# Quadrant matmuls for the token rows, and score blocks without the masked quarter, in a fused retention, expert and feed-forward kernel

## The chip, the core and the metric

The kernel runs on one core of a Trainium2 chip. The metric is device time in microseconds (us) from start to end of one execution; the median of several is quoted. The engines are named as the profile names them: PE is TensorE (PEld its weight loads), DVE VectorE, ACT ScalarE, POOL GpSimd, SP the engine that issues most DMAs.

## What is computed

Three layers in a row: a retention layer over 8 batches of 576 tokens with 8 heads of 64, a layer of 8 experts that sends each token to one expert, and a feed-forward layer with a cosine gate. The change lies in the first layer and in what leads from it into the second.

```python
scores = scale * np.matmul(q, k.transpose(0, 1, 3, 2))
Dmat = np.where(rel >= 0, gamma[:, None, None] ** rel[None, :, :], 0.0)
attn = np.matmul(scores * Dmat[None], v)                 # [B, H, S, 64]
x = attn.transpose(0, 2, 1, 3).reshape(B * S, H * 64)    # token rows
logits = x @ w_gate                                      # 8 experts
expert_idx = np.argmax(logits, axis=1)
# each token: relu(x @ w1[e]) @ w2[e], times the softmax weight of its expert
# then h = x @ w_in; (h * cos(h)) @ w_out
```

`rel` is the query's position less the key's, so of a block of 128 keys by 128 queries the entries with a key after the query are zero: below the diagonal nothing counts, and the quarter of the last 64 keys by the first 64 queries is zero as a whole.

## The kernel before

A batch of 576 tokens is cut into five chunks, four of 128 tokens and one of 64 (`CH`, `NCH` = 5), so the first layer is 40 steps, i = 0 to 39. A chunk's keys and queries lie turned (head dimension on the partitions), two heads on top of each other: partitions 0 to 63 hold the even head of a pair j, 64 to 127 the odd one. Per step the parts are:

- `load(i)` (L438 for a full chunk, 1 MB in one DMA; L440 and L441 for the half one) fills one of five `ld` buffers. It is issued on SP at the end of step i - 4, behind the store of the token rows, and its buffer comes free when `intra(i - 5)` has read it.
- `decay(i)` (L449): eight ACT multiplications, one a head, of the values v by the powers of gamma, into `vs`.
- `scores(i)` (L462): keys times queries, 16 matmuls of 64 rows by 64 columns and 128 moving columns (8 of 64 for a half chunk), spread over the array's four quadrants; the even heads go into one PSUM bank, the odd ones into another. DVE multiplies both by the mask into `pT` (L466).
- `inter(i)` (L487, not for a batch's first chunk): the state of the chunks before, `sbd`, times the queries. `intra(i)` (L497, L506): `vs` times `pT` into the same bank pair `xp`, DVE's multiplication into `xt` (L500), then the new state `S`, which ACT copies to `sbd` (L509).
- `rows(i)` (L518): 4 full-array matmuls with 136 moving columns, `xt` against `wgi`, which holds an identity and the gate's weights side by side. Out of it come the token rows (ACT copy `xs`, L520, then the store L523 into `xd`) and partial logits (DVE sum `lgt`, L521).
- `route`, `place`, `spread`, `table`: once per batch, the choice of an expert and the places of the tokens, on DVE, POOL and a little PE. The first expert's weights (`wst`, `wunit`) are loaded and split in the same steps 6 to 28.

Nothing reorders instructions: each engine runs them in the order in which the code emits them, and a step emits `scores(i)`, `decay(i + 1)`, `inter(i - 1)`, `intra(i - 1)`, `rows(i - 2)`, the routing, `load(i + 4)`. Scores and rows take turns in four PSUM banks (tag `sc`). Every fp32 matmul stands in the trace as two records, each with a weight load of its own; so 16 matmuls are 32 records.

At the start SP loads the first chunks in pieces, 13 matmuls on a cleared tile (`warm`, L211) run until the first chunk is there, and `wgi` is put together on DVE (L391 to L395).

## Time and profile before

| | us |
|---|---|
| median of 3 runs | 1379.56 (1375.28 to 1381.71) |
| profiled execution | 1377.58 |
| its span, first to last instruction | 1375.3 |
| PE busy | 1354.1 (98%) |
| DVE, ACT, POOL busy | 939.5 (68%), 757.2 (55%), 191.0 (14%) |
| DMA queue of SP | 256 MB, 53.0% of the 16 engines' span |

The span is one execution; the 2.3 us around it are start and end. PE's share is counted from records that overlap, so a busy PE can still be one that has less to do than its share says. The first layer ends at about 174 us, where the first expert's matmuls begin. From there PE is the engine that everything waits for. In the first layer PE, DVE, ACT and the DMA engines are all above three quarters, so there the shares alone don't tell which of them sets the pace.

### The profile page before, as it was taken

What the parts mean: (1) busy time and instruction counts of PE and PEld (TensorE: products, weight loads), DVE (VectorE), ACT (ScalarE), POOL (GpSimd) and SP (SyncE); (2) the same over time, 40 slices, a digit from 0 to 9 for tenths busy, and PEclk for the clock granted to TensorE, in tenths of its full rate; (3) what the DMA queues carried; (4) which work ended last, traced back from release to release, by engine and by line L of the source; (5) the groups of instructions that cost most, each with busy time, mean ns of one, the idle gap of its engine ahead of it and who ended that gap; (6) DMA issues with size and microseconds to landing.
All of it is one profiled execution on the core that took longest, in us unless ns stands there. A gap on an engine that the chain in (4) does not pass through costs nothing.

```text
span 1375.3 us, 28314 instructions
## 1 busy us (share of the span) xinstructions
PE 1354.1 (98%) x11234; PEld 1262.5 (92%) x11234; DVE 939.5 (68%) x1928; ACT 757.2 (55%) x1687; POOL 191.0 (14%) x300
## 2 busy tenths in 40 slices
PE   7999999999999999999999999999999999999998
PEld 6888899999999999998999999999999999999997
DVE  4777865867778687847666676766767676666655
ACT  5788725444544455336556555555555555555544
POOL 4334530121211212100010100101001010010101
PEclk9999999999999999999999999999999999999999
DMA  8899626575876668976564655646455564564551
GB/s 290 320 329 346 213 61 217 180 262 183 285 246 203 211 230 268 331 275 259 176 258 164 220 190 191 220 166 249 183 192 201 194 233 161 209 226 162 196 184 57
DMA packets 72648, 300.58 MB, mean 219 GB/s; under 512 B 7748, under 2 KB 15904, under 8 KB 58560
## 3 DMA queue, kind: packets, MB, share of 16 engines
q1 hardware_dynamic: 60000, 256.18, 53.0%
q0 software_dynamic: 12512, 42.56, 8.3%
q8 instruction: 89, 1.46, 0.4%
q14 instruction: 47, 0.39, 0.1%
HBM read 247.24 MB, written 51.47 MB: 217 GB/s over the span
## 4 chain that ended last, share of the span: by engine, by line
PE 49%; issue 6%; POOL 0%; POOLq 0%; ACT 0%
PE acc L1341 25%; PE hps L1265 24%; POOL out_dram L1323 0%; POOLq L1430 0%; ACT ka L1295 0%; POOL spare L159 0%; PE acc L1352 0%; POOLq L1323 0%; ACT orow L1321 0%
## 5 line engine op out<-in xcount | busy, mean ns | idle before, releaser
L1341 PE MATMUL acc<-wunit,gh 128*128 128x512 f32 x1152 | 358.2, 392 | 0.0
L1265 PEld LDWEIGHTS hps<-far,wquad 128*128 128x128 f32 x2064 | 261.8, 191 | 8.0 <-ACTq L1239 0.7
L1265 PE MATMUL hps<-far,wquad 128*128 128x256 f32 x2064 | 266.7, 283 | 0.5 <-ACTq L1239 0.5
L1341 PEld LDWEIGHTS acc<-wunit,gh 128*128 128x128 f32 x1152 | 207.2, 189 | 36.0
L1341 PE MATMUL acc<-wunit,gl 128*128 128x512 f32 x576 | 224.3, 389 | 0.0
L274 PE MATMUL hps<-xT,wunit 128*128 128x256 f32 (+6 forms) x1536 | 209.4, 297 | 0.5 <-ACT yev L291 0.5
L274 PEld LDWEIGHTS hps<-xT,wunit 128*128 128x128 f32 x1536 | 206.7, 188 | 0.9 <-ACT yev L291 0.7
L289 PE MATMUL hps<-hh,wunit 128*128 128x256 f32 (+6 forms) x960 | 197.9, 301 | 0.0
L289 PEld LDWEIGHTS hps<-hh,wunit 128*128 128x128 f32 x960 | 155.8, 190 | 0.1
L289 PE MATMUL hps<-hl,wunit 128*128 128x256 f32 (+6 forms) x480 | 143.5, 299 | 1.4 <-DVE hl L278 1.4
L1323 POOL DMA_INDIRECT out_dram<-orow,perm x36 | 35.4, 982 | 740.3 <-DVE orow L1319 736.4
L1341 PEld LDWEIGHTS acc<-wunit,gl 128*128 128x128 f32 x576 | 108.2, 188 | 24.5 <-DVE gl L1308 0.8
L1306 ACT CAST gh<-sa 128x512 fp32r<-128x512 f32 x144 | 89.6, 622 | 72.9 <-DVE sa L1302 72.9
L1302 DVE SCALAR_TENSOR_TENSOR sa<-sa,box 128x512 f32<-128x512 f32 x144 | 99.0, 688 | 42.8 <-ACT sa L1300 41.7
L1265 PE MATMUL hps<-near,wquad 128*128 128x256 f32 x960 | 126.6, 283 | 0.0
L1265 PEld LDWEIGHTS hps<-near,wquad 128*128 128x128 f32 x960 | 123.1, 191 | 3.6
L1276 DVE TENSOR_TENSOR box<-hps,box 128x256 f32<-128x256 f32 x72 | 30.6, 424 | 136.7 <-PE hps L1265 136.5
L1308 DVE TENSOR_TENSOR gl<-sa,gh 128x512 fp32r<-128x512 f32 x144 | 98.9, 687 | 18.5 <-ACT gh L1306 12.9
L1297 DVE SCALAR_TENSOR_TENSOR sa<-box,ka 128x512 f32<-128x512 f32 x144 | 98.9, 687 | 12.4 <-ACT ka L1295 12.3
L1275 ACT COPY box<-hps 128x256 f32<-128x256 f32 x72 | 26.8, 372 | 141.3 <-PE hps L1265 132.5
L1021 DVE TENSOR_TENSOR wunit<-wst,wunit 128x512 fp32r<-128x512 f32 x112 | 75.2, 686 | 36.9 <-ACT wunit L1020 36.8
L1299 ACT ACTIVATE sa<-sa 128x512 f32<-128x512 f32 x144 | 91.2, 634 | 8.6 <-DVE sa L1297 8.6
(217 smaller groups left out, 1877.4 us busy)
## 6 DMA issues: line engine op xcount, KB each, us to landing
wquad<-ws SPq DMA_DIRECT2D x72, 1792.0 KB
wst<-in_moe_w_dram SPq DMA_DIRECT2D x64, 512.0 KB
ld<-in_full_dram SPq DMA_DIRECT2D x29, 1024.0 KB
ws<-cvo POOLq DMA_DIRECT2D x28, 512.0 KB, 3.5
xd<-xs SPq DMA_DIRECT2D x32, 256.0 KB
cvw<-in_moe_w_in_dram SPq DMA_DIRECT2D x16, 512.0 KB
cvw<-in_moe_w_out_dram SPq DMA_DIRECT2D x16, 512.0 KB
wd<-cvo POOLq DMA_DIRECT2D x16, 512.0 KB, 5.3
```

Of the source, the lines that this page charges most:

```text
L274: mm(out=ph[:, :n], lhsT=u[:, a, kc, f0:f0 + P], rhs=t[:, bq, kc, :n], start=(idx == 0), stop=(idx == 11))
L289: mm(out=py[:, :n], lhsT=u[:, w], rhs=t[:, :n], start=(fc == 0 and g == 0), stop=(fc == 7 and g == 2))
L1021: nc.vector.tensor_sub(out=u[:, 1, 2 * g + c], in0=s[:, c], in1=u[:, 0, 2 * g + c])
L1265: mm(out=o, lhsT=u[:, s, kc, a], rhs=x[:, bq, kc], start=(s in (0, 1, 2) and idx == 0), stop=(idx == 5), skip_group_check=True)
L1276: nc.vector.tensor_add(out=u2, in0=y[:, :HT], in1=p1)
L1297: nc.vector.scalar_tensor_tensor(out=sa, in0=x, scalar=INV2PI, in1=ka, op0=ALU.mult, op1=ALU.subtract)
L1299: nc.scalar.activation(out=sa, in_=sa, func=AF.Sin, scale=math.pi)
L1302: nc.vector.scalar_tensor_tensor(out=sa, in0=sa, scalar=-1.0, in1=x, op0=ALU.add, op1=ALU.mult)
L1306: nc.scalar.copy(out=gh, in_=sa)
L1308: nc.vector.tensor_sub(out=gl, in0=sa, in1=gh)
L1323: ins = nc.gpsimd.indirect_dma_start(out=out[:, :], out_offset=bass.IndirectOffsetOnAxis(ap=perm[:, k:k + 1], axis=0), in_=o, in_offset=None)
L1341: mm(out=acc2[T][c], lhsT=pair[n][:, fh, c % 2 * P:(c % 2 + 1) * P], rhs=u[:, w, fc % 4], start=(q == 0 and fh == 0 and n == 0 and w == 0) ...
```

## The change

- `scores` of a full chunk leaves out the masked quarter: the last 64 keys are multiplied with the last 64 queries alone, 64 moving columns in place of 128. For every second pair of heads the two halves of the keys (and of the values and decays that belong to them) are swapped, on the host and in the tables, so that in each group of four matmuls all quadrants carry the same number of columns. The mask gets a second, swapped form. What stands in the quarter not written is multiplied by zero; so four named PSUM banks are cleared at the start and handed round (`next_bank`) in place of the pool's buffers.
- `rows` is done by head in the quadrants: 16 matmuls (8 for a half chunk) of 64 rows by 64 columns with 72 moving columns (64 of an identity and 8 of the gate) in place of 4 with 136. Token rows come out in plain head order, and the expert's first weights are laid in that order on the host. `wgi` is built on the host and loaded.
- `rows(i - 2)` is emitted right behind `decay(i + 1)`, ahead of `inter(i - 1)`; `rows(38)` ahead of `inter(39)`.
- `decay` is shared: from step 3 on, ACT does four heads one by one and POOL the other four in one instruction; for the first three chunks DVE does all eight in one, in the step itself.
- At the start the load of chunk 1's keys and queries goes ahead of chunk 0's values, a one-element ACT instruction brings the table load forward, and six more `warm` matmuls follow `scores(0)`.

```diff
...
+        banks = [ps1.tile([P, 4, P], F32, name=f"bank{i}") for i in range(4)]
+        for t in banks:
+            nc.vector.memset(t, 0.0)
+        def next_bank():
+            banks.append(banks.pop(0))
+            return banks[-1]
...
         def decay(i):
-            for h in range(H):
+            h0 = 0 if i < OWN else H // 2
+            for h in range(h0):
                 nc.scalar.mul(vs[:n, h], s["v"][:n, h], cc(C_GK + c * H + h, 1, n))
+            (nc.vector if i < OWN else nc.gpsimd).tensor_tensor(
+                out=vs[:n, h0:], in0=s["v"][:n, h0:],
+                in1=cc(C_GK + c * H + h0, H - h0, n).unsqueeze(2).to_broadcast([n, H - h0, D]), op=ALU.mult)
...
-            scs = [ps1.tile([P, 4, P], F32, tag="sc", name="sc", bufs=4) for g in range(2)]
+            scs = [next_bank() for g in range(2)]
...
+                for j0 in (0, 2):
+                    for late in range(2):
+                        for j in (j0, j0 + 1):
+                            r = D * (j % 2 ^ late)
+                            for g in range(2):
+                                mm(out=scs[g][r:r + D, j, D * late:], lhsT=kT[D * g:D * g + D, j, r:r + D],
+                                   rhs=qT[D * g:D * g + D, j, D * late:], start=(j0 == 0 and not late), stop=True,
+                                   skip_group_check=True)
...
         def rows(i):
+            two = [next_bank().rearrange("p j t -> p (j t)")[
+                :, :4 * RW].rearrange("p (j f) -> p j f", f=RW) for g in range(2)]
+            for j in range(4):
+                for g, r in ((0, 0), (1, D), (0, D), (1, 0)):
+                    if r < n:
+                        mm(out=two[g][r:r + D, j, :], lhsT=xt[D * g:D * g + D, j, r:r + D],
+                           rhs=wgi[D * g:D * g + D, j, :], start=(j == 0), stop=True, skip_group_check=True)
             for g in range(2):
-                two = ps1.tile([P, 4, P], F32, tag="sc", name="rw", bufs=4).rearrange("p (j a) t -> p j (a t)", a=2)
-                for j in range(2):
-                    mm(out=two[:, j, 0:RW], lhsT=xts[i % 3][:, 2 * g + j, :], rhs=wgi[:, 2 * g + j, :], start=(j == 0),
-                       stop=True, skip_group_check=True)
-                for j in range(2):
-                    mm(out=two[:, j, 0:RW], lhsT=xts[i % 3][:, 2 * g + j, :], rhs=wgi[:, 2 * g + j, :], start=(j == 0),
-                       stop=True, skip_group_check=True)
...
             scores(i)
-            if i + 1 < NS:
+            if i < OWN:
+                decay(i)
+            if i == 0:
+                warm(NWARM // 2, blank, idle)
+            if OWN <= i + 1 < NS:
                 decay(i + 1)
-            if i == 1:
-                setup_rows()
+            if i >= 2:
+                rows(i - 2)
...
             if i >= 1:
                 inter(i - 1)
                 intra(i - 1)
...
-            if i >= 2:
-                rows(i - 2)
```

On PE, one full step as it stood before: scores, state, values, new state, and the token rows last.

```order
L462 MATMUL sc<-ld 64x128 x16
L487 MATMUL xps<-ld,sbd_136 64x128 x8
L497 MATMUL xps<-pT,vs 64x128 x8
L506 MATMUL S<-vs,ld 64x64 x8
L518 MATMUL rw<-wgi,xt_130 128x136 x4
L462 MATMUL sc<-ld 64x64 x8
```

On PE now, the piece from the end of a step's rows (L566) to the scores of the next step, a half one (L494).

```order
L566 MATMUL bank_149<-wgi,xt_131 64x72
L566 MATMUL bank_150<-wgi,xt_131 64x72
L532 MATMUL xps<-ld,sbd_136 64x128 x8
L542 MATMUL xps<-pT,vs 64x128 x8
L551 MATMUL S<-vs,ld 64x64 x8
L494 MATMUL bank_147<-ld 64x64
L494 MATMUL bank_148<-ld 64x64
```

The rows now stand between scores and state, so the new state is followed at once by the next scores, and rows of chunk i - 2 wait for DVE's `xt` of the step just before.

On DVE, a step with `spread` before: masks, `xt`, the sums of the logits, then the spread's small instructions.

```order
L466 TENSOR_TENSOR pT<-sc,ca 128x4x128 x2
L500 TENSOR_TENSOR xt_132<-xps,gx 128x512
L521 TENSOR_REDUCE lgt_140<-rw 128x8 x2
L605 TENSOR_REDUCE rm<-dd 128x5
L618 TENSOR_REDUCE gts<-ex 128x5
```

The same step on DVE now.

```order
L511 TENSOR_TENSOR pT<-bank_147,ca 128x4x128
L511 TENSOR_TENSOR pT<-bank_148,ca 128x4x128
L570 TENSOR_REDUCE lgt_139<-bank_149 128x8
L570 TENSOR_REDUCE lgt_139<-bank_150 128x8
L545 TENSOR_TENSOR xt_131<-xps,gx 128x512
L654 TENSOR_REDUCE rm<-dd 128x5
```

The sums of the logits, which wait for ACT's copies, have moved ahead of `xt`.

On POOL, once per batch, the chain of the placing before.

```order
L584 TENSOR_TENSOR dd<-dd,hot 128x200
L608 TENSOR_SCALAR tokc<-ct 128x5
L609 TENSOR_TENSOR rt<-hot,tokc 128x5x40
L612 TENSOR_SCALAR oh<-ca,rm 128x128 x5
L626 TENSOR_TENSOR rt<-hot,gh 128x5x40
L626 TENSOR_TENSOR rt<-hot,gl 128x5x40
L575 TENSOR_TENSOR dd<-dsts,ca 128x200
```

The same place on POOL now.

```order
L633 TENSOR_TENSOR dd<-dd,hot 128x200
L478 TENSOR_TENSOR halfv_142<-ld,ca 64x256
L657 TENSOR_SCALAR tokc<-ct 128x5
L658 TENSOR_TENSOR rt<-hot,tokc 128x5x40
L661 TENSOR_SCALAR oh<-ca,rm 128x128 x5
L675 TENSOR_TENSOR rt<-hot,gh 128x5x40
L675 TENSOR_TENSOR rt<-hot,gl 128x5x40
L478 TENSOR_TENSOR vs<-ld,ca 128x256 x4
```

POOL's halves of `decay` (L478) stand between the pieces of that chain.

## Rows read from the trace of the kernel before

**Rows 1.** Windows of 100 us, 170 to 1370 us, their sum: length, busy time.

```profile
sum 1200.00, PE 1195.48 PEld 1120.88 DVE 820.16 ACT 630.83 POOL 117.44; mean PE 99.62 PEld 93.41 DVE 68.35 ACT 52.57 POOL 9.79
```

**Rows 2.** Windows, one per batch of five steps: length, busy, PEclk, DMA share, GB/s.

```profile
28.97:47.61 18.64, 18.64 (x400) 16.98 (x399) 14.19 (x47) 13.84 (x53) 5.83 (x11) 1.00 0.90 315
47.61:70.20 22.59, 20.38 (x406) 17.98 (x405) 15.82 (x47) 16.86 (x63) 7.85 (x15) 1.00 0.91 324
...
89.99:109.79 19.80, 19.55 (x405) 17.68 (x405) 15.73 (x47) 16.54 (x59) 8.53 (x16) 1.00 0.92 326
109.79:129.48 19.69, 19.69 (x405) 17.75 (x405) 15.72 (x47) 16.30 (x59) 8.34 (x15) 1.00 0.97 351
129.48:148.97 19.50, 19.50 (x406) 17.70 (x406) 15.93 (x51) 16.19 (x59) 8.14 (x15) 1.00 0.88 306
```

**Rows 3.** Timeline of PE, one full step: start, length, line, tiles, shape, records.

```profile
102.04 1.10 PE L462 MATMUL sc<-ld 64*64 64x128 f32 x32
102.96 0.62 PE L487 MATMUL xps<-ld,sbd 64*64 64x128 f32 x16
103.51 1.09 PE L497 MATMUL xps<-pT,vs 128*64 128x128 f32 x16
104.44 0.64 PE L506 MATMUL S<-vs,ld 128*64 128x64 f32 x16
105.00 1.19 PE L518 MATMUL rw<-wgi,xt 128*128 128x136 f32 x8
106.12 0.27 PE L462 MATMUL sc<-ld 64*64 64x64 f32 x2
```

**Rows 4.** Narrow windows, L462 (128 columns), then L487 (64): (x) is records in flight.

```profile
109.98:110.00 0.02, 0.02 (x8) 0.02 (x6) 1.00 0.99 410
110.08:110.10 0.02, 0.02 (x12) 0.02 (x8) 1.00 0.26 102
...
110.73:110.75 0.02, 0.02 (x4) 0.02 (x8) 1.00 0.97 410
110.85:110.87 0.02, 0.02 (x12) 0.02 (x11) 1.00 0.00 0
```

**Rows 5.** Groups of instructions, 109.79 to 129.48: count, busy, mean ns, idle before.

```profile
L466 DVE TENSOR_TENSOR pT<-sc,ca 128x512 f32<-128x512 f32 x8 | 5.1, 678 | 0.0
L521 DVE TENSOR_REDUCE lgt<-rw 128x8 f32<-128x16 f32 (+1 forms) x10 | 1.7, 173 | 3.4 <-ACT xs L520 3.4
L449 ACT ACTIVATE vs<-ld,ca 128x64 f32<-128x64 f32 x32 | 8.1, 338 | 1.5 <-DMA ld<-in_full_dram 1.5
L520 ACT COPY xs<-rw 128x256 f32<-128x256 f32 (+1 forms) x11 | 4.1, 371 | 1.0 <-PE rw L518 0.2
L584 POOL TENSOR_TENSOR dd<-dd,hot 128x200 f32<-128x200 f32 x1 | 0.6, 610 | 0.1
```

**Rows 6.** The window of 4 us with the highest rate.

```profile
84.00:88.00 4.00, 4.00 (x84) 3.63 (x82) 3.53 (x12) 3.29 (x13) 3.58 (x8) 1.00 1.04 408
```

**Rows 7.** Timeline: two loads' issues and the decays that waited for them; waits, 20 to 160 us.

```profile
49.49 1.33 SPq L438 DMA_DIRECT2D ld<-in_full_dram  x1
60.46 0.82 ACT L449 ACTIVATE vs<-ld,ca 128x64 f32<-128x64 f32 x3 [3.57 <-DMA ld<-in_full_dram]
...
110.71 0.38 SPq L438 DMA_DIRECT2D ld<-in_full_dram  x1
118.82 2.02 ACT L449 ACTIVATE vs<-ld,ca 128x64 f32<-128x64 f32 x8 [1.06 <-DMA ld<-in_full_dram]
...
ACT vs L449 <- DMA ld<-in_full_dram: 13.6, 12, 3.6
```

**Rows 8.** Timeline of the start.

```profile
0.87 1.45 POOL L405 MEMSET xt<- 128x512 f32 x3
...
18.98 2.02 ACT L449 ACTIVATE vs<-ld,ca 128x64 f32<-128x64 f32 x8 [1.01 <-DMA ld<-in_full_dram]
...
22.15 0.62 PE L487 MATMUL xps<-ld,sbd 64*64 64x128 f32 x16
```

## The prediction

> **What bounds the kernel now.** I read the windows first, then the timeline of one step, then the waits of the engines next to PE.

> Behind the first layer PE is busy 1195.5 of 1200 us [rows 1], and the change does not touch what it does there. So what the first layer saves or loses goes one to one into the end. The base of the sum is the profiled execution, 1377.58 us; the median of the runs is 1379.56, 0.14% above it. A measurement of this kernel can tell about 0.5% from no change: below 1372.7 is faster, above 1386.5 slower.

> In the first layer the windows of a batch [rows 2] show that PE has no idle time in the fifth and sixth batch (19.69 of 19.69, 19.50 of 19.50), and .25 in the fourth; the granted clock is 1.00, even in the second batch, where PE was idle for 2.2 us. So PE sets the pace. Close behind come ACT (16.3 of 19.7), DVE (15.7) and the DMA engines (.88 to .97, 306 to 351 GB/s). That is the case in which a faster PE soon meets something else. Seven batches start between 28.97 and about 168.5; the third, between the second's end and the fourth's start, took 19.8, and the seventh I take as the sixth. Sum: 18.64 + 22.59 + 19.80 + 19.80 + 19.69 + 19.50 + 19.50 = 139.5 us. The second is 2.8 us longer than its like.

> **PE's part.** A full step takes 4.08 us from scores to scores: scores .92, state .55, values .93, new state .56, rows 1.12 [rows 3].

> Records in the quadrants start four together. With 128 moving columns the next four follow about .10 us later (from 8 to 12 in flight in .10); with 64 columns two fours come in .12, so .06 a four [rows 4]. The new scores of a full chunk are 4 fours with 128 columns and 4 with 64, so 4 x (.11 - .06) = .2 us go, .92 becomes .72. The new rows are 8 fours (16 matmuls, two records each) with 72 columns. By .06 x 72/64 a four costs .064, eight cost .51 instead of 1.12, so .61 go. A half chunk's scores don't change; its rows I count like a full one's, since the old ones were 4 full matmuls too. Per batch 4 x .2 + 5 x .61 = 3.85: PE alone would need 19.69 - 3.85 = 15.84 us. Eight batches give 31 us, the most PE can return.

> Moving `rows` next to `scores` also puts two quadrant shapes side by side. I count nothing for it. There are a quarter more PE instructions in a step (records 176 before, 224 now); no row has a price for fetching them, and I bound it by nothing and the 2.8 us of the second batch.

> [...]

> **DVE.** Its masks, `xt` and sums keep their sizes. A batch has 15.7 us of them, and the 3.4 us that it idles ahead of `lgt` it spends waiting for ACT's `xs` [rows 5]. With small gaps the floor is 16.0 to 16.2 us, just above PE's 15.84. In the new order `lgt` stands ahead of `xt`, and `rows(i - 2)` waits for the `xt` of the step just before. So ACT's `xs`, which stands behind `decay`, which waits for a load, now reaches PE by way of DVE within a step.

> **ACT and POOL.** Half the decays leave ACT: (8.1 for full chunks + 2.0 for the half one)/2 = 5.05 us a batch, leaving 11.3 of 16.3 busy. POOL takes them: a row of 128 x 200 takes .61 [rows 5], so 128 x 256 some .78, and 5 of them 3.9 on 8.3, far from full. Only the chain of the placing gets longer: `rm` on DVE waits for POOL's `dd`, which now may stand behind one decay. Bound: nothing, or one POOL decay (.78) a batch, 5 us in all, if DVE has no slack; I take nothing, as DVE waits for ACT anyway, and keep the 5 for the range.

> **The loads.** The highest rate of the trace is 408 GB/s in 4 us at a share of 1.04 [rows 6]. A batch that also carries two loads of `wst` moves 19.69 x 351 = 6.91 MB (the first, third and fifth of the seven), one with a single `wst` load 6.45 (second, fourth), one without 5.97 (sixth, seventh). At 408 the heavy one takes 16.9 us; at the 351 that it reached, 19.7. So the bytes alone leave room for 2.8 us or for none.

> What decides is latency. `load(i + 4)` can go only when the new state of chunk i - 1 has read its buffer, at the end of step i. The timeline has a load whose issue took from 110.71 to 111.09, and whose decay started at 118.82, having waited for it 1.06 us: L = 7.7 us behind the issue. ACT waited 12 times for such loads, 13.6 us together [rows 7]; before, this was off the path. Behind the landing now come, in step i + 3 and ahead of `rows(i + 2)` in step i + 4: half a decay, about 1.0 (2.02 for eight), two `xs` copies .75 (371 ns), two sums .35 (173 ns), `xt` .68 (like `pT`) [rows 5, 7], 2.8 in all; with the issue (.38) 3.2, with hand-offs 3.3. The scores of that step (.72) lie in between in the change's favour; I leave them as reserve. Three steps must hold it: 3T = L + 3.3. With L = 7.7 T is 3.67 and a heavy batch 18.3 us. I scale L with a batch's bytes: 7.2 and 17.5 for a medium batch, 6.65 and 16.6 for a light one. The heavy one then moves 378 GB/s, inside what [rows 6] shows.

> **The start.** Four cleared banks stand ahead of the tile that `warm` reads. Clearing 128 x 512 three times took 1.45 us on POOL. But the first steps wait for loads: the decay of chunk 3 starts at 18.98, when its load is there, and the third step's state matmuls start at 22.15 [rows 8]. The new order of the first loads helps chunk 0, not chunk 3. I take a gain of .6 (one step's rows), with -1.0 and +2.9 as bounds: the loss if chunk 3's load lands later by as much as ACT waits for it there (1.01), the gain if the clearing now beside it (twice 1.45) came free.

> **The sum.** 3 x 18.3 + 2 x 17.5 + 2 x 16.6 = 123.1 against 139.5, a gain of 16.4. The second batch keeps its stall, so 2.8 come back. Start .6, and the last two rows 2 x .61 = 1.2. 1377.6 - 16.4 + 2.8 - .6 - 1.2 = **1362.2 us**. L half a us shorter or longer moves T by .17, thus 35 steps by 6 us: 1356 to 1368.

> **Rivals.** *A, the forecast*: loads set the pace through ACT and DVE. For it: the twelve waits. Chance .50.

> *B, loads keep up and DVE sets the pace*: 7 x 16.2 = 113.4, a gain of 26.1 and 1.8 for start and end, 1350. For it: 408 GB/s in [rows 6], and a load issued sooner may land sooner. Against it: the heavy batches would have to hold 426 GB/s for 16.2 us. PE alone would end at about 1346. Chance .23.

> *C, loads don't come faster at all*: heavy batches stay at 19.7, medium at 19.8, light ones fall to 17.0 (5.97 MB at 351). Gain 5.0 + 1.8: 1371. For it: shares of .97 and above, where the queue is full. Against: [rows 6]. Chance .15.

> *D, the change doesn't shorten the records*: their starts have a least distance, and fewer columns don't bring them closer. The scores' 32 records in .92 are 29 ns each. If that were such a floor, scores would save nothing, rows 1.12 - .92 = .20, PE's batch be 18.7, and eight batches with the start give 1369. Against it: 15 ns in [rows 4]. Chance .06. [...]

> *E, slower*: PE used to pass over a late load, since rows stood a whole step behind `xt`; now `lgt` ahead of `xt` and the closer `rows` carry it to PE. This decides where L exceeds 3 x 4.08 - 3.3 = 8.9. One load was issued by 50.82 and its decay ran at 60.46, L = 9.6, ACT having idled 3.57 [rows 7]; if L stayed there, T would be 4.3, 35 steps would lose .2 each, and the end be 1385; with L = 10, 1390. Against it: that was a single load in the batch with the stall; 7.7 is more like the others. Chance .06.

> **How the numbers follow.** A has the largest chance: 1362. The range takes in B's nearer edge and C: 1348 to 1371; outside are D's and E's slow ends and the half of B in which PE's pace is met. Faster by the bound: nearly all of A, B and D, and two thirds of C, .87; the same: the rest of C, an E with L near 9, .08; slower: E, .05.

> **What would show it.** [...] Batches of 16.6 to 18.3 us, heavy ones longer than light ones, PE idle 1 to 2.5 us in them, DVE's idle still ahead of `lgt`, ACT waiting for `ld` (A). All batches at 16.2 with DVE busy throughout (B). Heavy batches unchanged at 350 GB/s with a share of 1 (C). PE idle, steps above 4.08 (E). Wrong would be the forecast above all if L is not fixed but shrinks with less queueing, or if POOL's halves hold up `vs` or `rm`: then waits on POOL would head DVE's or PE's list.

## The result, and the profile after

The changed kernel takes **1398.51 us** (median of 4 runs, 1396.05 to 1401.81) beside 1378.40 of the kernel before on the same chip: ratio 1.0132, interval 1.0111 to 1.0154. It is 20 us slower; the forecast was 1362, the range 1348 to 1371. The profiled execution has a span of 1400.0 us against 1375.3, so 24.7 us stand to be explained in it.

Where they lie shows in the start of each batch's first new state (first record of `S`, L506 before and L551 now; the last state is taken at the last record of `S`):

| | before | after | more |
|---|---|---|---|
| from the start to the second batch's `S` | 33.94 | 38.05 | 4.1 |
| six batches, second to eighth | 121.0 (20.2 each) | 135.8 (22.6 each) | 14.8 |
| from there to the last state | 13.4 | 16.1 | 2.7 |
| from the last state to the end | 1207.0 | 1210.1 | 3.1 |

The first view is the windows of four batches in a row, as in [rows 2]: length, busy time of PE, PEld, DVE, ACT and POOL with counts, PEclk, DMA share, GB/s.

```profile
63.70:87.20 23.50, 19.29 (x514) 17.61 (x512) 16.53 (x47) 11.14 (x38) 11.15 (x19) 0.85 0.83 293
87.20:109.70 22.50, 18.78 (x514) 17.13 (x510) 16.20 (x47) 11.13 (x38) 11.26 (x19) 0.87 0.77 283
109.70:131.80 22.10, 18.04 (x510) 16.49 (x508) 16.66 (x47) 11.13 (x38) 11.21 (x19) 0.90 0.85 295
131.80:154.90 23.10, 19.15 (x512) 17.55 (x510) 16.26 (x47) 11.14 (x38) 11.17 (x19) 0.86 0.81 291
```

No engine is full any more, the DMA engines move less per second than before, and the granted clock, 1.00 in every batch of [rows 2], is .85 to .90: part of each batch ran at half of it. In the windows of 81 to 86, 105 to 110, 128 to 131 and 149 to 154 us it is .50. What PE waits for is in the list of its waits, 20 to 180 us (total, times, longest):

```profile
PE bank L566 <- issue: 14.8, 6, 3.2
PE bank L494 <- issue: 10.2, 7, 2.2
PE S L551 <- issue: 1.6, 1, 1.6
PE bank L566 <- DVE xt L545: 1.6, 1, 1.6
```

"issue" is time in which PE waits for nothing that the profile shows: 26.6 us in 14 gaps. Only one gap is a wait for `xt`. The timeline of PE shows such a gap and what follows (start, length, line, tiles, shape, records, idle before):

```profile
99.51 0.41 PE L566 MATMUL bank<-wgi,xt 64*64 64x72 f32 x10
102.62 0.54 PE L566 MATMUL bank<-wgi,xt 64*64 64x72 f32 x20 [2.70 <-issue]
...
104.05 1.51 PE L686 MATMUL lg<-rt,oh 128*128 128x120 f32 x5
105.48 1.56 PE L505 MATMUL bank<-ld 64*64 64x128 f32 x32
106.81 1.17 PE L566 MATMUL bank<-wgi,xt 64*64 64x72 f32 x16
107.92 1.97 PE L542 MATMUL xps<-pT,vs 128*64 128x128 f32 x16
```

PE stops in the middle of a line, after 10 of 32 records whose operands are all there, for 2.7 us; then the same lines take nearly twice as long as at a granted clock of 1.00, the values 1.97 us where they take 1.10 below. The gap is one cost, the half clock that follows a second. A step without a gap is as the forecast had it:

```profile
114.19 0.90 PE L505 MATMUL bank<-ld 64*64 64x128 f32 x32
114.91 0.68 PE L566 MATMUL bank<-wgi,xt 64*64 64x72 f32 x32
115.42 0.62 PE L532 MATMUL xps<-ld,sbd 64*64 64x128 f32 x16
115.96 1.10 PE L542 MATMUL xps<-pT,vs 128*64 128x128 f32 x16
116.89 0.64 PE L551 MATMUL S<-vs,ld 128*64 128x64 f32 x16
117.45 0.33 PE L494 MATMUL bank<-ld 64*64 64x64 f32 x4
```

Scores .72, rows .51, the whole step 3.26 us against 4.08 [rows 3]. PE's arithmetic did become faster by what was claimed. (One slip ahead of the prediction: token rows don't come out in plain head order but in the array's, with the heads of pairs 1 and 3 swapped; the first weights are laid to match.)

### The profile page after: what moved, and what is told of

It is laid out like the page before. It is cut to its first block, busy times and chain, and to the rows that moved or that the text cites. A ratio compares the mean times of both kernels' runs of the same rounds, so it can differ in the third digit from the quotient of the medians.

```text
span 1400.0 us, 29955 instructions
## 1 busy us (share of the span) xinstructions
PE 1345.9 (96%) x12072; PEld 1255.3 (90%) x12072; DVE 946.9 (68%) x1931; ACT 713.5 (51%) x1516; POOL 211.3 (15%) x334
## 4 chain that ended last, share of the span: by engine, by line
PE 48%; issue 5%; POOL 0%; POOLq 0%; ACT 0%
PE acc L1390 25%; PE hps L1314 23%; POOL out_dram L1372 0%; POOLq L1481 0%; ACT ka L1344 0%; POOL spare L188 0%; PE acc L1401 0%; POOLq L1372 0%; ACT orow L1370 0%
## 5 line engine op out<-in xcount | busy, mean ns | idle before, releaser
L303 PE MATMUL hps<-xT,wunit 128*128 128x256 f32 (+6 forms) x1440 | 197.5, 298 | 1.1 <-DVE hl L307 0.6
L303 PEld LDWEIGHTS hps<-xT,wunit 128*128 128x128 f32 x1440 | 195.2, 188 | 1.8 <-DVE hl L307 1.1
L1314 PEld LDWEIGHTS hps<-near,wquad 128*128 128x128 f32 x960 | 123.1, 191 | 3.6
```

Source lines behind the costliest of these rows:

```text
L303: mm(out=ph[:, :n], lhsT=u[:, a, kc, f0:f0 + P], rhs=t[:, bq, kc, :n], start=(idx == 0), stop=(idx == 11))
L1314: mm(out=o, lhsT=u[:, s, kc, a], rhs=x[:, bq, kc], start=(s in (0, 1, 2) and idx == 0), stop=(idx == 5), skip_group_check=True)
```

## The experiments

**Theory F** (fetch): PE's instructions come through the DMA engines in blocks, in turn with the loads; the changed kernel eats a block faster than the next one comes. **Theory R**: the rival of the prediction's slow side, late loads carried to PE by the closer chain `decay`, `xs`, `lgt`, `xt`, `rows`. The kernel before is measured beside each group; its medians there are 1380.25 (first four), 1380.16 (next four) and 1380.75 (last four).

### Rows as full-array matmuls again (rows_full)

```diff
...
-                        mm(out=two[g][r:r + D, j, :], lhsT=xt[D * g:D * g + D, j, r:r + D],
-                           rhs=wgi[D * g:D * g + D, j, :], ...)
...
+                    mm(out=two[:, j, 0:RW], lhsT=xt[:, 2 * g + j, :], rhs=wgi[:, 2 * g + j, :], ...)
...
```

> The changed kernel with one part undone: the token rows are again 4 full-array matmuls with 136 columns (identity of 128 and gate), everything else (short scores, order, shared decays, banks) as changed. A full step then has 88 matmul records in place of 112. Theory F (PE's instruction stream is loaded in blocks of about 127 matmul records, and in the changed kernel PE eats a block faster than the next one comes through the loaded DMA engines): the gaps of 2 to 3 us that PE has in the middle of L566 and L494 with nothing to wait for (25 us between 20 and 180) nearly vanish, the granted clock goes back to 1.00 in the layer, and the time falls below before, to 1365 to 1378. Theory R (late loads reach PE over decay, xs, lgt, xt and the closer rows): order and decays are those of the change, so the steps stay above 4.1 us and the time stays at 1390 to 1400.

Measured: 1380.59, ratio 1.0008 (.9993 to 1.0023). Giving back 24 records a step takes away the whole loss, although each step's rows now last .6 us longer. The clock is back at 1.00 and the last three full batches take 19.4 to 19.5 us; the first of them:

```profile
95.80:115.20 19.40, 19.40 (x410) 17.32 (x406) 15.95 (x48) 11.34 (x38) 11.50 (x20) 1.00 0.95 333
```

R is against this, F for it, though the time lies 2.6 us above F's range. Two things in the trace go that way. Next to full-array rows the scores don't take .72:

```profile
106.39 0.67 PE L532 MATMUL xps<-ld,sbd 64*64 64x128 f32 x16
106.99 1.09 PE L542 MATMUL xps<-pT,vs 128*64 128x128 f32 x16
107.91 0.63 PE L551 MATMUL S<-vs,ld 128*64 128x64 f32 x16
108.48 0.90 PE L505 MATMUL bank<-ld 64*64 64x128 f32 x32
109.30 0.38 PE L564 MATMUL bank<-wgi,xt 128*128 128x136 f32 x1
```

From 108.48 to 109.30 it is .82, and the state takes .60 where it took .55: the two changes of shape cost .15 of the .2. And the first batch (23.9 us from `S` to `S`, 20.5 before) and the last chunks (17.0 us, 13.4 before) lose more than the six batches between gain (118.2 us, 121.0 before). Why they do was not tested.

### Scores with 128 columns again (scores_full)

```diff
...
-                                mm(out=scs[g][r:r + D, j, D * late:], ..., rhs=qT[D * g:D * g + D, j, D * late:], ...)
...
+                        mm(out=scs[g][r:r + D, j, :], ..., rhs=qT[D * g:D * g + D, j, :], ...)
```

> The changed kernel with the other part undone: scores again with 128 columns in all 16 matmuls (keys, values and mask stay swapped). As many matmul records as in the changed kernel. Theory F: a block of instructions lasts a little longer (.2 us a step), so the gaps of PE shrink by what the scores cost: 1393 to 1404, no change that can be measured. If the short score records themselves were the trouble: 1385 or less. Theory R: the .2 us a step lie beside the late loads: no change.

Measured: 1398.56, ratio 1.0119 (1.0088 to 1.0151), the changed kernel's time within its interval. PE works .2 us a step longer and the time does not move: its gaps shrink in turn (9.3 + 4.5 us in eight gaps between 60 and 153 us; 9.6 + 6.4 in the same eight in the changed kernel, 63.7 to 154.9), and six batches take 135.9 us as against 135.8. Here PE's own speed neither costs nor buys anything. R expects the same here, so this run speaks against the short records as the trouble, not for F over R.

### Rows as 8 matmuls of 64 by 128 (rows_half)

```diff
-                for g, r in ((0, 0), (1, D), (0, D), (1, 0)):
...
-                        mm(out=two[g][r:r + D, j, :], lhsT=xt[D * g:D * g + D, j, r:r + D], ...)
+                for g in range(2):
+                    mm(out=two[g][:n, j, :], lhsT=xt[D * g:D * g + D, j, :n], ...)
```

> The changed kernel with the rows as 8 matmuls of 64 rows by 128 columns with 72 moving columns, two at a time, in place of 16 in the quadrants: about the same array time, 96 matmul records a step in place of 112. Theory F: a block lasts 4.4 us in place of 3.7, the gaps of PE get shorter by some .6 us each or miss a boundary altogether: 1380 to 1392. Theory R: 1395 to 1400, as the changed kernel.

Measured: 1390.13, ratio 1.0079 (1.0051 to 1.0107), within F's range and below R's. But the rows were not as short as assumed:

```profile
83.23 1.11 PE L565 MATMUL bank<-wgi,xt 64*128 64x72 f32 x16
84.27 0.67 PE L532 MATMUL xps<-ld,sbd 64*64 64x128 f32 x16
```

1.04 us for 16 records with 72 columns, 65 ns each, where a full-array record with 136 columns takes 140 (1.12 us for 8, [rows 3]). By its columns such a record alone would take 74 ns, an estimate, and two side by side would make that 37. By that the two row halves of the array did not work side by side here. So a block lasted longer for that reason too, and "issue" falls to 2.9 us in three gaps between 53 and 155 us. The six batches from second to eighth take 116.6 us, less than before (121.0); in the profiled execution the loss lies ahead of them (39.3 us to the second batch's `S`, 33.9 before) and behind them. The run agrees with F without weighing much.

### The kernel before with 12 tiny matmuls more a step (before_pad)

```diff
+                if n == P:
+                    for a, r in ((0, 0), (0, D)) * 3:
+                        mm(out=two[r:r + D, 1, RW:RW + 4], lhsT=xts[i % 3][D * a:D * a + D, 2 * g + 1, r:r + D],
+                           rhs=wgi[D * a:D * a + D, 2 * g + 1, 0:4], start=False, ...)
```

> The kernel before, with 12 tiny matmuls (64 by 64, 4 moving columns) added behind the full chunks' rows, into a part of the bank that nobody reads: 112 matmul records a step as in the changed kernel, order, loads and decays as before. Direct cost on PE by 15 to 29 ns a record .36 to .7 us a step, 12 to 23 us in all if PE sets the pace. Theory F: on top of that gaps of PE in mid-line with nothing to wait for, 10 us or more of them between 20 and 180, and stretches with the clock below 1.00. Theory R: the direct cost alone, no such gaps beyond the 2 to 3 us of the kernel before.

Measured: 1411.85, ratio 1.0222 (1.0199 to 1.0244). F's expectation failed: as many records as in the changed kernel, and no gap. The padding itself was dearer than thought:

```profile
93.70 0.52 PE L522 MATMUL rw<-wgi,xt 64*64 64x4 f32 x12
94.14 0.73 PE L518 MATMUL rw<-wgi,xt 128*128 128x136 f32 x4
94.80 0.52 PE L522 MATMUL rw<-wgi,xt 64*64 64x4 f32 x12
```

12 records in .44 us, 37 ns each with 4 columns; a step became 5.2 us long (90.08 to the routing at 95.25). 112 records in 5.2 us are 127 in 5.9 us, as slow as before the change. So it isn't the count of records in a step that decides but the records per us. F was worded too simply here; R's "direct cost alone" holds. The run also speaks against a cause in the number of records alone.

### The same program, shifted by 64 instructions (shift)

```diff
             if i == 0:
                 warm(NWARM // 2, blank, idle)
+                for _ in range(SHIFT):    # SHIFT = 64
+                    mm(out=blank[:, :4], lhsT=idle.bitcast(BF16)[:, :P], rhs=idle.bitcast(BF16)[:, :4], ...)
```

> The changed kernel with 64 tiny matmuls (4 columns) more on the cleared tile behind scores(0), while PE waits for the first values. Nothing else differs in the layer, but each block of instructions now ends 64 records earlier in the program. Theory F: the gaps of PE leave their fixed places (inside L494 and L566) and turn up 64 records earlier, that is in the lines ahead of those (inside L551, L542 or L532 of the steps ahead), about two a batch; time within 1% of the changed kernel's, 1385 to 1405. Theory R, or any cause that lies in the data of L494 or L566 (a bank not free, xt late): the gaps stay in L494 and L566.

Measured: 1390.38 (1.0059, 1.0041 to 1.0077). Here the count of PE's records from the start to a gap decides. First the changed kernel, windows from 0 to the starts of three of its gaps (length, PE busy with count, PEclk, DMA share, GB/s):

```profile
0.00:52.94 52.94, 38.06 (x982) 0.94 0.83 294
0.00:71.42 71.42, 53.31 (x1363) 0.90 0.80 282
0.00:77.32 77.32, 57.15 (x1489) 0.91 0.81 292
```

Then the shifted one, three of its gaps:

```profile
0.00:49.02 49.02, 35.84 (x982) 0.93 0.91 312
0.00:64.17 64.17, 48.04 (x1362) 0.95 0.92 313
0.00:88.79 88.79, 67.72 (x1870) 0.92 0.89 304
```

The gaps stay behind record 982, 1362 or 1363, 1870 (in the changed kernel one lies behind 1869), though 64 of the records ahead of them are new. In the changed kernel the gaps in mid-line lie behind records 855, 982, 1363, 1489, 1869, 1996, 2376, 2503, 2883, 3009, with 126 or 127, or three times that, between them. Those of the shifted one lie on the same grid: behind 855, 982, 1362, 1870, 2377, 2883. In the program they have moved, as the timeline of the gap behind record 1362 shows, in the changed kernel first:

```profile
71.02 0.62 PE L494 MATMUL bank<-ld 64*64 64x64 f32 x13
73.70 0.33 PE L494 MATMUL bank<-ld 64*64 64x64 f32 x3 [2.06 <-issue]
```

```profile
63.71 0.68 PE L567 MATMUL bank<-wgi,xt 64*64 64x72 f32 x29
67.27 0.28 PE L567 MATMUL bank<-wgi,xt 64*64 64x72 f32 x2 [2.88 <-issue]
```

There it cut the half chunk's scores (L494), here the rows of the step before. No operand, bank or semaphore can do that; only the place in PE's stream of instructions can. Which lines would be hit was guessed wrong (rows again, and scores L506, rather than states and values).

The DMA view has what comes in this rhythm: between 47.69 and 145.30 PE ran records 856 to 3010, some 17 times 127, and the queue of instructions moved

```profile
q8 instruction: 17, 0.28, 1.1%
```

that is 17 packets of 16 KB. The gap behind record 1996 starts at 99.70; its packet starts between 99.9 and 100.4, in a stretch in which other transfers took 105% of the engines' time:

```profile
q1 hardware_dynamic: 53, 0.22, 104.8%
q8 instruction: 1, 0.02, 12.3%
```

All ten gaps between 47.69 and 147.5 us are of this kind. The packet for the next block takes .9 to 1.0 us, but starts only 2.7 to 4.8 us after PE entered the block before it, and PE goes on 1.3 to 1.5 us after it has landed. The block that it had, it ran through in 3.6 to 3.8 us.

So not every crossing from one block to the next cost PE a stop: the 17 packets go with 10 gaps of 1.2 to 3.4 us (from the start of one record to the start of the next).

### Rows at the end of the step again (rows_last)

```diff
-            if i >= 2:
-                rows(i - 2)
             if i >= 1:
                 inter(i - 1)
                 intra(i - 1)
...
+            if i >= 2:
+                rows(i - 2)
```

> The changed kernel with the order alone undone: rows(i - 2) again behind the new state and the routing, at the end of a step, and rows(38) behind intra(39). Records, loads, decays and the start as changed. Theory F: as many records in as little time, so the gaps of PE stay, at other lines; 1390 to 1402. Theory R (the closer rows carry late loads to PE): gaps gone, 1365 to 1380.

Measured: 1397.56, ratio 1.0145 (1.0118 to 1.0172). The order is undone and nothing is gained; PE's waits from 55 to 168 us are again

```profile
PE bank L494 <- issue: 13.0, 5, 3.6
PE xps L532 <- issue: 7.8, 4, 2.9
```

R falls as the cause of the loss in the batches.

### A quarter less to load, then nothing to load (light_load, no_load)

```diff
-                for a0, a1 in parts or ((0, 4),):
+                for a0, a1 in parts or ((0, 3),):
...
-                s["v"], s["k"] = [... for a in (2, 3)]
+                s["v"], s["k"] = [... for a in (2, 2)]
```

> The changed kernel with 25% less in each full chunk's load: the keys by token (256 KB of 1 MB) are not loaded, and the state is computed from the values in their place, so that part of the result is another one. PE's instructions are the same, record for record. Theory F: the blocks of instructions no longer stand behind so much in the DMA engines; PE's gaps in L494 and L566 shrink from 1.2 to 3.4 us to under 1, the clock stays at 1.00, batches of 17 to 19 us, 1365 to 1380. A rival by which the number of records alone slows PE (decoding, weight loads) expects the gaps to stay and 1392 to 1400.

```diff
+            if i >= 5:
+                s.update({key: st[i - 5][key] for key in ("ld", "kT", "qT", "v", "k")})
+                return
```

> The changed kernel in which from the second batch on no chunk is loaded: every batch uses the first batch's keys, queries and values again, so that the result and all that follows the first layer are others; only the first layer's stretch up to about 170 us counts. PE's instructions are the same. Theory F, as light_load left it (25% less load shortened the gaps to 0.7 to 2.7 us but did not end them): with the DMA engines nearly empty a block comes 3.6 us after the one before was begun, and PE's gaps fall to at most .5 us, batches of 16 to 17 us in place of 22 to 23.5. If the gaps stay at 1 us or more, a block's own latency and not the load traffic makes them.

Both route tokens in another way, so their whole times (1661 and 1685 us) say nothing; only the first layer counts. With a quarter less the batches take 18.5 to 22.5 us in place of 22.1 to 23.5, and "issue" falls from 19.2 us (53 to 155 us in the changed kernel) to 11.0 (52 to 150). Some two fifths went, not nearly all as expected, and single gaps of up to 2.4 us stayed. Without loads the batches take 17.1 to 19.8 us, not the 16 to 17 expected, two of them

```profile
69.00:86.70 17.70, 16.17 (x510) 14.92 (x508) 14.89 (x46) 10.91 (x38) 11.90 (x19) 0.98 0.30 100
86.70:106.50 19.80, 17.93 (x514) 16.19 (x512) 17.21 (x50) 10.96 (x38) 11.89 (x19) 0.93 0.34 117
```

and PE's waits from 49 to 142 us hold no "issue" at all:

```profile
PE lg L689 <- POOL rt L678: 6.9, 5, 1.5
PE bank L508 <- DVE pT L514: 1.0, 6, 0.2
```

The same 510 records a batch, the same instructions, no traffic of loads, no gaps. From 49.2 to 142.2 us the queue of instructions brought 20 packets, one each 4.65 us, and the list above holds no stop for one; with the loads it had one each 5.7 us (97.6 us for 17) and ten gaps. So the loads hold up the instructions; with shift and the packets' times in the changed kernel, F is shown. What is left is the next limit: each batch PE's `lg` waits for POOL's `rt`, 1.4 us on the average, and in two of four batches, the ones of 19.8 us, the granted clock was .93 (.98 in those of 17.7 and 17.8).

### Short scores alone, and what the start costs (scores_only, scores_warm, before_warm)

scores_only is the kernel before with the scores, masks and banks of the change and nothing else of it.

> The kernel before with the short scores alone (swapped halves, second mask, four cleared banks handed round), and its own order, rows, decays and start. 88 records a full step, as before. Theory F: a block lasts 127 / 88 x 3.9 = 5.6 us, so no more gaps than before; scores save .2 us in 32 steps, 6.4 us: 1370 to 1376. If the short records cost a gap or a switch of shapes instead: 1377 to 1383.

Measured: 1377.76, ratio .9980 (.9967 to .9993), 2.4 us faster where 4 to 10 were expected. Its last three full batches take 19.1 us against 19.5 to 19.7, but the first takes 23.7 against 20.5. The timeline of PE there:

```profile
18.58 1.13 PE L520 MATMUL xps<-ld,sbd 64*64 64x128 f32 x16 [3.01 <-ACT sbd L542]
19.64 1.98 PE L530 MATMUL xps<-pT,vs 128*64 128x128 f32 x16
```

With a gap of 3.0 us for `sbd` the clock fell, and the lines ran at half speed until 24 us (the rows 1.98 us from 22.40 in place of 1.19; from 24.31 the scores took .72 again); before, with a gap of 2.7 in the same place, it did not: the granted clock from 14 to 28 us is 1.00, the values from 18.61 take 1.09. Each is one execution. 20 matmuls on the cleared tile now fill it:

```diff
             scores(i)
+            if i == 2:
+                warm(20, banks[0].rearrange("p j t -> p (j t)"), idle)
```

> The kernel before with the short scores alone, as scores_only, and 20 matmuls on the cleared tile behind scores(2), into a bank that is free then, while PE waits 3 us for the state. In scores_only the clock fell behind that gap and the next steps ran at half speed until 24 us, 2.5 us lost. If that is the reason for its slow first batch (23.7 against 20.5 us), the first batch takes 20.5 to 21.5 and the time is 1373 to 1376; if the first batch is slow for its loads, 1377 to 1379.

> The kernel before with the same 20 matmuls at the same place and nothing else: what they do by themselves. In the profiled run of before the clock had not fallen there, so nothing in such an execution: 1379 to 1381; if it falls in part of the executions, up to 2 us less.

scores_warm: **1376.52**, ratio .9969 (.9955 to .9984), 4.2 us below before, the lowest median of all and half a us above the expected range. before_warm: 1378.93, .9988 (.9972 to 1.0004), nothing that can be told from none. The clock stays up in the profiled execution of scores_warm,

```profile
18.55 0.67 PE L520 MATMUL xps<-ld,sbd 64*64 64x128 f32 x16 [0.31 <-ACT sbd L542]
19.14 1.09 PE L530 MATMUL xps<-pT,vs 128*64 128x128 f32 x16
```

its first batch takes 20.2 us, and the short scores are worth 2.4 us without the filling (1380.16 to 1377.76) and with it (1378.93 to 1376.52). What the filling itself is worth is not shown: the intervals of scores_only and scores_warm overlap.

### Half of the decays on POOL (scores_pool)

```diff
-            for h in range(H):
+            h0 = H if i < OWN else H // 2
+            for h in range(h0):
                 nc.scalar.mul(vs[:n, h], s["v"][:n, h], cc(C_GK + c * H + h, 1, n))
+            if h0 < H:
+              nc.gpsimd.tensor_tensor(out=vs[:n, h0:], in0=s["v"][:n, h0:], ...)
```

> As scores_warm, and from chunk 3 on half of the decays on POOL, as in the changed kernel: one more part of the change by itself. ACT's 16.9 us of 19 become 11.5, but PE sets the pace, so the time is that of scores_warm within 2 us; if POOL's halves hold up vs or the placing, 2 to 5 us more.

Measured: 1378.17, ratio .9984 (.9971 to .9996), 1.7 above scores_warm with intervals that overlap. From 75 to 155 us PE waits for the placing in every batch,

```profile
PE lg L676 <- POOL rt L665: 3.8, 4, 1.0
```

where scores_warm's row for the same wait is 1.3 us in 3 times. But the batches don't take longer for it: six of them 119.7 us, 120.1 in scores_warm. So a price of POOL's halves is not shown. ACT idles more (busy 11.9 us from 94.3 to 114.0, 16.6 in scores_warm) and nobody needs it.

## Why the prediction was wrong

- **What failed** is one sentence: "There are a quarter more PE instructions in a step (records 176 before, 224 now); no row has a price for fetching them, and I bound it by nothing and the 2.8 us of the second batch." The bound was for the whole kernel; the cost came about twice in every batch. In the batch from 87.2 to 109.7 the gaps are 1.2 and 2.9 us (start to start), and a clock of .87 over 22.5 us loses another 2.9, an estimate. With the 15.84 us of PE's own work that makes 22.8; measured are 22.5. By this estimate all of the loss of a batch, and the expected gain with it, is in these two terms.
- **The row for it was there.** The second batch of [rows 2] was 2.8 us too long, and the prediction spoke of a stall, and in rival E of a late load. Some 1.9 us of it were the first case of this kind, 10 of 16 records into `S`:

```profile
58.67 0.51 PE L506 MATMUL S<-vs,ld 128*64 128x64 f32 x10
60.85 0.39 PE L506 MATMUL S<-vs,ld 128*64 128x64 f32 x6 [1.67 <-issue]
```

  The packet for PE's next block had started 6.1 us after PE entered the block before, at 58.27; PE went on 1.5 us after its landing. In the kernel before 405 records took 19.7 us, so 127 lasted 6.2 us, and this was the only such gap between 53 and 155 us. The forecast's 16.6 to 18.3 us for 510 records asked for one every 4.1 to 4.6 us. Measured: 5.6 with all loads (22.6 us), 4.6 to 5.6 with a quarter less. The records per us stood in [rows 3]; they were not divided by what brings them.
- **PE's part** was right to the hundredth in a step without a gap: scores .72, rows .51, that is 22 and 16 ns a record, below the 29 that rival D took for a floor. Rival D falls. The change of shapes, counted as nothing, costs nothing there, but .15 us a step next to full-array rows (rows_full).
- **DVE, ACT**: DVE 16.2 to 16.7 busy a batch (forecast a floor of 16.0 to 16.2), ACT 11.1 (11.3). **POOL**: 11.2 (12.2); its half decay took .61, not .78.
- **The loads** as the pace (forecast A): not reached. The DMA engines moved 283 to 295 GB/s in place of 306 to 351; PE waited for instructions, not for them. Whether 378 GB/s could be held stays untested.
- **POOL's halves**, taken as nothing with 5 us as bound: PE's wait for the placing grew by .6 us a batch in scores_pool, (3.8 - 1.3)/4, without longer batches, and is 1.4 in no_load, where the halves' part in it was not tested; in the changed kernel it doesn't show. So "nothing" is not refuted, but the path was another one: not `rm` on DVE but `rt`, which PE's `lg` needs.
- **The start**, a gain of .6: it lost 4.1. A first gap for instructions (.9 us) stands at 17.0, in `S`. Step 3 shows rival E's mechanism at work once: ACT stood 6.5 us for chunk 3's load with `xs` behind it, `xt` went at 21.13 and the rows at 21.96; rows, state and values then ran at half clock (granted .50 from 22 to 25 us), and a second gap for instructions (2.4 us) came at 26.5. How much each cost stays open: kernels with nearly the same start reached the second batch's `S` at 32.6 (rows_last), 35.6 (shift) and 36.9 us (scores_full).
- **Rival E** had the sign and nearly the time (1385 to 1390), for another reason: rows_last shows that the order is not it. That it came near was luck. The range was too narrow because no case held a limit of PE's instructions, which is none of the engines, waits or transfers that I had listed.
- The last 2.7 and 3.1 us, the end of the layer and what is behind it, were not tested; the second is within what single executions differ by (1206 to 1211 us in the kernels here that route as before, but for before_pad with 1215).

## What to carry to other kernels

Here the rows, cut from 4 matmuls into 16 that run side by side, took .51 us in place of 1.12 and had 24 records more; with such a cut, count records per us before and after, and look whether PE already has gaps in the middle of a line with nothing to wait for (the kernel before had one of 1.67 us). With the loads on the DMA engines at 283 to 295 GB/s PE went no faster here than its blocks came, 5.7 us each, and a gap of 2.7 us cost a second time, as the clock fell to .50 behind it. Parts of a change should be timed apart: here short scores alone gained .2%, the change without the quadrant rows nothing that can be told from none, and the quadrant rows made it a loss of 1.3%.
